# A fused attention and mixture-of-experts kernel: v of the odd early steps in the output's buffers, v of the late steps through scratch in HBM and turned as float32r

## The chip, the cores and the metric

The kernel runs on one core of one Trainium2 chip. The metric is the device time of one execution in microseconds. Three runs of the kernel before took 1270.45, 1270.66 and 1270.89 us; their median, 1270.66 us, is the number that the prediction is about. The engines are PE (matrix products), with PEld for its weight loads, ACT, DVE and POOL (elementwise work; POOL also issues the indirect transfers), and SP, which issues the plain transfers on one hardware queue.

## The reference, cut to what matters

```
# q, k, v: B=4, N=5056, C=256, float32
qn = q / (norm(q, axis=1) + 1e-6);  kn = k / (norm(k, axis=1) + 1e-6)
s  = kn.transpose(0, 2, 1) @ qn / tau            # 256 x 256 for each batch
a  = softmax(s, axis=-1)
x  = (v @ a).reshape(20224, 256)
logits = x @ w_gate + modality_bias[modality_id]  # 8 experts
e_idx  = argmax(logits, axis=1);  gate = softmax(logits)[e_idx]
for e in range(8):
    h = maximum(x[e_idx == e] @ w1[e], 0)         # 256 -> 1024
    out[e_idx == e] = gate * (h @ w2[e])          # 1024 -> 256
```

The norms and the scores sum over all tokens of a batch, so a batch's x can start only when its q and k have been read whole. A token's expert is known only when its x is there.

## The kernel before, in words

**Steps.** Each batch is cut into 10 steps of 512 tokens (the tenth is shorter), 40 steps in all, numbered g = 10 b + s. Most products are made of three float32r matmuls, high by high, low by high and high by low, where the high part is a float32r cast made by ACT and the low part the rest, subtracted by DVE.

**Gram.** `kq_pieces(b, s)` loads q and k of a step (L291), makes high and low parts (L307, L308), squares both for the norms (ACT L333, summed into acc by DVE at L335) and multiplies k by q into two PSUM banks (L344 for whole float32 operands, as in the first batch and steps 0 to 4 of batch 1; L358 and L362 for split ones). Batch 0's gram is done first, the next batch's beside the current one's steps.

**v times a.** `va_pieces(b, s)` loads v of the step (L542) into a tile with the tag "v", of which there are two buffers. `tr(h)` turns one half of the channels: four 128 x 128 transposes on PE (L559, with a float32 identity `ident`) fill one PSUM tile vtp, ACT casts it to vh (L563), DVE subtracts to vl (L564). `av(t)` multiplies (L577, 24 matmuls a step) and ACT copies the result to x (L581). `route()` finds the expert of each token (DVE L586 to L636, exp on ACT L592, the tokens' ranks by three small matmuls into rp, L613 to L615), and POOL scatters the rows of x to the list xs in HBM, sorted by expert (L499).

**Blocks.** 512 tokens of one expert are a block: weights loaded (w1r L738, w2r L742) and split (L759, L766), rows xr read back from xs (L719), turned (xtp L778, with the float32r identity `identr`), then the first product hp (L796, 12 matmuls for each of 8 parts), its relu as hh (ACT L799) and hl (DVE L800), the second product y (L814) and the scaled result yo (L830), scattered to the output by POOL (L499). yo has two buffers with the tag "yo"; the first block's yo is made after step 6.

**Order.** The pieces of a step (a block's body, v of the next step with the routing of this one, the next batch's gram) are merged by `_interleave` in the order written, and the tiling framework then sets each engine's queue by what depends on what. Instructions that depend on nothing are put early. `order(ins, others)` and `after(...)` name instructions that must come behind others; kq_pieces takes such a list as `behind`, and for batch 1's early steps it is `routed[g]`, the last instructions of a step's routing. In a queue nothing overtakes: a waiting instruction holds up what is behind it. SP issues every load of q, k, v, w1r, w2r and xr in one such order.

## Time and profile before

| | |
|---|---|
| runs, median (lowest to highest) | 1270.66 us (1270.45 to 1270.89) |
| the profiled execution | 1268.5 us |
| its span | 1266.7 us |
| PE busy | 1231.8 us, 97% of the span |
| DVE, ACT, POOL busy | 66%, 59%, 28% |
| mean granted clock of PE | 0.995 of full speed |
| hardware DMA queue (SP's loads) | 167.61 MB, 41.8% of the 16 DMA engines' time |

The profile is of one execution; its span is the time from the first to the last instruction that it shows. Rows of groups give line, engine, operation, tiles (out<-in), shapes and count, then busy time and the mean ns of one, then the idle time of the engine before them and what ended it. Rows of a timeline give start and duration in us. "x4" stands for four instructions in a row; their duration reaches from the start of the first to the end of the last, and since matmuls overlap in the pipeline, the step from one start to the next is what a stream pays. SPq is SP's queue of transfers.

### The profile page before, as it was taken

To read this page: it belongs to the slowest core of one execution; us is meant where nothing else is said; L and a number is where in the kernel's file an instruction comes from. 1 tells how busy PE (TensorE), PEld (TensorE's weight loads), DVE (VectorE), ACT (ScalarE), POOL (GpSimd) and SP (SyncE) were. 2 spreads that over 40 slices of the span, in tenths; PEclk is the share of its full clock that TensorE was granted. 3 is DMA by queue.
4 is the path that set the end of the run, shared out by engine and by line. 5 is a ranking of instruction groups with operands and counts; after the bars stand their busy time and mean duration, and the time that the engine had idled before them with its cause. 6 is when DMAs were issued, how large, how long until landed. Compare 5 with 4: busy or idle time off the path is not lost.

```text
span 1266.7 us, 23483 instructions
## 1 busy us (share of the span) xinstructions
PE 1231.8 (97%) x8226; PEld 1113.8 (88%) x8226; DVE 836.7 (66%) x2196; ACT 743.1 (59%) x1519; POOL 358.1 (28%) x344
## 2 busy tenths in 40 slices
PE   9989999999999999999999999999999999989997
PEld 8878899888988889889998998888888888879997
DVE  6788688676667766677776776565556655465452
ACT  6656568666666566676665665564555455444553
POOL 0053333222332223213332322222222333233121
PEclk9999999999999999999999999999999999999999
DMA  8869465455554555545555554434444454334320
GB/s 314 294 201 322 141 205 186 162 167 167 180 180 163 175 176 188 166 139 194 174 173 184 173 176 138 143 103 150 150 154 147 136 156 146 129 115 143 121 97 28
DMA packets 104177, 210.82 MB, mean 166 GB/s; under 512 B 11336, under 2 KB 52808, under 8 KB 104048
## 3 DMA queue, kind: packets, MB, share of 16 engines
q1 hardware_dynamic: 88304, 167.61, 41.8%
q0 software_dynamic: 15744, 41.61, 8.5%
q8 instruction: 66, 1.08, 0.4%
q14 instruction: 63, 0.52, 0.1%
HBM read 167.06 MB, written 43.43 MB: 166 GB/s over the span
## 4 chain that ended last, share of the span: by engine, by line
PE 83%; issue 8%; DVE 3%; DMA 2%; ACT 1%; POOL 1%; POOLq 0%; SPq 0%; ACTq 0%; DVEq 0%
PE y L814 30%; PE hp L796 29%; PE xp L577 10%; PE g L344 3%; PE g L358 3%; PE vtp L559 3%; PE g L362 2%; PE xtp L778 2%; DMA k<-in_k_dram 1%; POOL out_dram L499 1%; DVE hl L800 1%; DMA v<-in_v_dram 1%; PE ns L395 1%; ACT hh L799 1%; DVE acc L335 0%
## 5 line engine op out<-in xcount | busy, mean ns | idle before, releaser
L499 POOL DMA_INDIRECT xs<-x,pi x160 | 181.4, 1134 | 749.0 <-ACT w1h L759 483.1
L814 PE MATMUL y<-w2h,hh 128*128 128x256 f32 x1264 | 358.4, 284 | 6.4 <-ACT hh L799 5.2
L814 PE MATMUL y<-w2h,hl 128*128 128x256 f32 x1264 | 353.7, 280 | 2.6 <-DVE hl L800 2.2
L814 PE MATMUL y<-w2l,hh 128*128 128x256 f32 x1264 | 353.5, 280 | 0.1
L800 DVE SCALAR_TENSOR_TENSOR hl<-hp,hh 128x512 fp32r<-128x512 f32 (+1 forms) x320 | 217.0, 678 | 181.6 <-ACT hh L799 154.5
L799 ACT ACTIVATE hh<-hp 128x512 fp32r<-128x512 f32 (+1 forms) x320 | 189.9, 594 | 218.0 <-PE hp L796 147.5
L796 PE MATMUL hp<-xh,w1h 128*128 128x512 f32 (+1 forms) x640 | 256.4, 401 | 4.1 <-issue 4.1
L814 PEld LDWEIGHTS y<-w2h,hh 128*128 128x128 f32 x1264 | 237.8, 188 | 22.1 <-ACT hh L799 9.3
L796 PE MATMUL hp<-xl,w1h 128*128 128x512 f32 (+1 forms) x640 | 251.4, 393 | 0.9 <-issue 0.6
L796 PE MATMUL hp<-xh,w1l 128*128 128x512 f32 (+1 forms) x640 | 250.7, 392 | 0.3 <-issue 0.3
L814 PEld LDWEIGHTS y<-w2l,hh 128*128 128x128 f32 x1264 | 238.3, 189 | 9.2
L814 PEld LDWEIGHTS y<-w2h,hl 128*128 128x128 f32 x1264 | 237.1, 188 | 5.8 <-DVE hl L800 4.6
L499 POOL DMA_INDIRECT out_dram<-yo,xr x158 | 164.1, 1039 | 127.4 <-ACT yo L830 82.2
L766 DVE TENSOR_TENSOR w2l<-w2r,w2h 128x512 fp32r<-128x512 f32 x160 | 110.3, 689 | 66.9 <-ACT w2h L759 60.6
L796 PEld LDWEIGHTS hp<-xh,w1l 128*128 128x128 f32 x640 | 120.3, 188 | 27.2 <-issue 1.5
L759 ACT CAST w2h<-w2r 128x512 fp32r<-128x512 f32 x160 | 99.6, 622 | 70.3 <-PE y L814 54.9
L766 DVE TENSOR_TENSOR w1l<-w1r,w1h 128x512 fp32r<-128x512 f32 x160 | 110.3, 689 | 43.8 <-ACT w1h L759 37.6
L796 PEld LDWEIGHTS hp<-xl,w1h 128*128 128x128 f32 x640 | 120.7, 189 | 19.4 <-issue 5.4
L796 PEld LDWEIGHTS hp<-xh,w1h 128*128 128x128 f32 x640 | 120.4, 188 | 15.7 <-issue 2.4
L759 ACT CAST w1h<-w1r 128x512 fp32r<-128x512 f32 x160 | 100.1, 626 | 50.6 <-PE hp L796 47.0
L577 PE MATMUL xp<-ah,vh 128*128 128x264 f32 x320 | 97.7, 305 | 1.7 <-issue 0.8
L577 PE MATMUL xp<-al,vh 128*128 128x264 f32 x320 | 92.1, 288 | 0.7 <-issue 0.7
(154 smaller groups left out, 1750.3 us busy)
## 6 DMA issues: line engine op xcount, KB each, us to landing
w1r<-in_moe_w_dram SPq DMA_DIRECT2D x80, 512.0 KB
w2r<-in_moe_w_dram SPq DMA_DIRECT2D x80, 512.0 KB
xr<-xs SPq DMA_DIRECT2D x38, 516.0 KB
v<-in_v_dram SPq DMA_DIRECT2D x36, 512.0 KB
q<-in_q_dram SPq DMA_DIRECT2D x35, 512.0 KB
k<-in_k_dram SPq DMA_DIRECT2D x35, 512.0 KB
xs<-x,pi POOLq DMA_INDIRECT x160
out_dram<-yo,xr POOLq DMA_INDIRECT x158
```

Source lines behind the costliest of these rows:

```text
L344: nc.tensor.matmul(g[:, 0:C], st["k"][:pp, 2 * h + t, m * P : (m + 1) * P], st["q"][:pp, 2 * h + t, :], start=first, stop=last, skip_group ...
L358: nc.tensor.matmul(g, ks[:pp, t, m * P : (m + 1) * P], qs[:pp, t, :], start=first, stop=False, skip_group_check=True,)
L362: nc.tensor.matmul(g[:, 0:C], ks[:pp, t, C + m * P : C + (m + 1) * P], qs[:pp, t, 0:C], start=False, stop=last, skip_group_check=True,)
L499: ins = nc.gpsimd.indirect_dma_start(out=dst, out_offset=bass.IndirectOffsetOnAxis(ap=idx, axis=0), in_=rows, in_offset=None, bounds_check ...
L559: nc.tensor.matmul(tp[:, t * P : (t + 1) * P], st["v"][:, t, h * P : (h + 1) * P], ident, is_transpose=True, start=t == 0, stop=True, skip ...
L577: nc.tensor.matmul(xp[:, 0:DE], a[:, h, t * P : (t + 1) * P], w[:, h, :], start=i == 0, stop=i == len(seq) - 1,)
L759: ins = nc.scalar.copy(hi, src).ins
L766: nc.vector.tensor_tensor(lo, src, hi.bitcast(F32), ALU.subtract)
L796: nc.tensor.matmul(hp[:, 0:rows], w[:, h, fs], x[:, h, 0:rows], start=i == 0, stop=i == len(seq) - 1)
L799: nc.scalar.activation(hh[:, 0:rows], hp[:, 0:rows], AF.Relu)
L800: nc.vector.scalar_tensor_tensor(hl[:, 0:rows], hp[:, 0:rows], 0.0, hh[:, 0:rows].bitcast(F32), ALU.max, ALU.subtract)
L814: ins = nc.tensor.matmul(y, a[:, tsl], w[:, j % 2, :], start=(j == 0 and i == 0 and t % 2 == 0), stop=(j == NJ - 1 and i == 2), skip_group ...
```

## The change

It has three parts.

1. The v tile of an odd step below 6 (v_1, v_3, v_5) takes the tag "yo", the buffers of the output, which are free until the first block; the even ones keep "v".
2. `routed[g]` also holds the exp of the routing, and batch 1's gram pieces are put behind the cast and the subtraction of a turned v (`turned[...]`) as well as behind the routing.
3. For steps 12 to 39 `stage(g)` has SP copy v of the step from the input to a scratch tensor `vs{g}` in HBM, and the load reads that scratch. The tile of v is then float32r by type, and so is the PSUM tile; the transposes use `identr`. The bytes are the same; the cast and the subtraction read the PSUM tile as float32.

```diff
     cast = {}
+    turned = {}
...
+    staged = set(range(NS + 2, G))
+    vs = {
+        g: dram.tile([parts(g % NS) * TT, C], F32, name=f"vs{g}") for g in sorted(staged)
+    }
+
+    def stage(g):
+        b, s = divmod(g, NS)
+        n = parts(s) * TT
+        nc.sync.dma_start(
+            vs[g].rearrange("(p t) c -> p t c", t=TT),
+            v[b, s * STEP : s * STEP + n, :].rearrange("(p t) c -> p t c", t=TT),
+        )
...
         def load():
-            vt = p2.tile([P, TT, C], F32, tag="v", name=f"v_{g}")
+            dt = F32R if g in staged else F32
+            vt = p2.tile([P, TT, C], dt, tag="yo" if g % 2 == 1 and g < first_block else "v", name=f"v_{g}")
...
-            nc.sync.dma_start(
-                vt[:pp], v[b, t0 : t0 + pp * TT, :].rearrange("(p t) c -> p t c", t=TT)
-            )
+            src = vs[g] if g in staged else v[b, t0 : t0 + pp * TT, :]
+            nc.sync.dma_start(vt[:pp].bitcast(F32), src.rearrange("(p t) c -> p t c", t=TT))
...
-                tp = ps2.tile([P, 512], F32, tag="h" if early else "aux", name=f"vtp_{g}_{h}")
+                dt = F32R if g in staged else F32
+                tp = ps2.tile([P, 512], dt, tag="h" if early else "aux", name=f"vtp_{g}_{h}")
             for t in range(TT):
                 nc.tensor.matmul(
-                    tp[:, t * P : (t + 1) * P], st["v"][:, t, h * P : (h + 1) * P], ident,
+                    tp[:, t * P : (t + 1) * P], st["v"][:, t, h * P : (h + 1) * P], identr if g in staged else ident,
                     is_transpose=True, start=t == 0, stop=True, skip_group_check=True,
                 )
-            cast[g] = nc.scalar.copy(st["vh"][:, h, :], tp).ins
-            ins = nc.vector.tensor_tensor(st["vl"][:, h, :], tp, st["vh"][:, h, :].bitcast(F32), ALU.subtract)
+            tf = tp.bitcast(F32) if g in staged else tp
+            cast[g] = nc.scalar.copy(st["vh"][:, h, :], tf).ins
+            turned.setdefault(g, []).append(("act", cast[g]))
+            ins = nc.vector.tensor_tensor(st["vl"][:, h, :], tf, st["vh"][:, h, :].bitcast(F32), ALU.subtract)
...
+            turned[g].append(("dve", ins.ins))
...
-            nc.scalar.activation(ex, lm, AF.Exp)
+            exps = nc.scalar.activation(ex, lm, AF.Exp)
...
             routed[g] = [
+                ("act", exps.ins),
...
-            run(kq_pieces(1, s, lambda: routed[0], squares[s]))
+            run(kq_pieces(1, s, lambda: routed[0] + turned[1], squares[s]))
...
-                streams.append(list(kq_pieces(1, 2, lambda: routed[1], squares[2])))
+                streams.append(list(kq_pieces(1, 2, lambda: routed[1] + turned[2], squares[2])))
             else:
-                streams.append([f for i in (PLAN[s] if b == 0 else [s]) for f in kq_pieces(b + 1, i, routed[g - 1] if b == 0 and g > 0 else ())])
+                streams.append([f for i in (PLAN[s] if b == 0 else [s]) for f in kq_pieces(b + 1, i, routed[g - 1] + turned[g] if b == 0 and g > 0 else ())])
+        if g + 4 in staged:
+            streams[-1].insert(len(streams[-1]) // 2, lambda g=g: stage(g + 4))
```

What this does to the queues shows at three places. In the rows a number is a row's place in its engine's queue, and the last number of a tile's name is the program's own.

SP in the early steps, first before and then in the change, from the load of v_5 to the first weights of block 0 (w1r_0_0) and the first x rows (xr_0):

```order
46 L542 DMA v_5_1034<-in_v_dram 128x1024
47 L542 DMA v_6_1196<-in_v_dram 128x1024
48 L734 TENSOR_LOAD pki_0_896
...
51 L738 DMA w1r_0_0_1177<-in_moe_w1_dram 128x2x512
...
53 L742 DMA w2r_0_0_1178<-in_moe_w2_dram 128x4x256
...
57 L719 DMA xr_0_1190<-xs_129 128x1032
...
59 L738 DMA w1r_0_1_1192<-in_moe_w1_dram 128x2x512
```

```order
45 L560 DMA v_6_1224<-in_v_dram 128x1024
46 L291 DMA q_1_5_1429<-in_q_dram 128x1024
47 L291 DMA k_1_5_1431<-in_k_dram 128x1024
48 L540 DMA vs12_131<-in_v_dram 16x8192
49 L560 DMA v_7_1412<-in_v_dram 128x1024
50 L540 DMA vs13_132<-in_v_dram 16x8192
51 L540 DMA vs14_133<-in_v_dram 16x8192
52 L755 TENSOR_LOAD pki_0_924
...
55 L759 DMA w1r_0_0_1205<-in_moe_w1_dram 128x2x512
...
61 L740 DMA xr_0_1218<-xs_129 128x1032
```

v_7, which stood behind the weights of blocks 0 and 1, now stands ahead of them, with the first three copies (vs12 to vs14) around it.

SP ahead of batch 2's first q and k (q_2_0, k_2_0), where the last copies stand, before and in the change:

```order
133 L719 ISA
134 L719 DMA xr_4_2642<-xs_129 128x1032
135 L738 ISA
136 L738 DMA w1r_5_0_3102<-in_moe_w1_dram 128x2x512
137 L734 TENSOR_LOAD pki_6_2612
...
141 L291 DMA q_2_0_3174<-in_q_dram 128x1024
142 L291 DMA k_2_0_3176<-in_k_dram 128x1024
143 L542 DMA v_12_3641<-in_v_dram 128x1024
```

```order
156 L740 DMA xr_4_2671<-xs_129 128x1032
157 L540 DMA vs34_153<-in_v_dram 16x8192
158 L540 DMA vs35_154<-in_v_dram 16x8192
159 L540 DMA vs36_155<-in_v_dram 16x8192
160 L540 DMA vs37_156<-in_v_dram 16x8192
161 L540 DMA vs38_157<-in_v_dram 16x8192
162 L540 DMA vs39_158<-in_v_dram 16x7168
...
164 L759 DMA w1r_5_0_3132<-in_moe_w1_dram 128x2x512
165 L291 DMA q_2_0_3199<-in_q_dram 128x1024
...
170 L291 DMA k_2_0_3201<-in_k_dram 128x1024
...
173 L560 DMA v_12_3672<-vs12_131 128x1024
```

All 28 copies stand between rows 48 and 162, one to six at a place, though the program writes them four steps ahead of each use: nothing that they read is written by the kernel.

ACT from the second x copy of step 2 on, before and in the change (vh_4 is the cast of step 4's v, ex_2 the exp of step 2's routing, sq_1_3 are the squares of batch 1's step 3):

```order
87 L581 COPY x_2_675<-xp_2_2_826 128x264
88 L581 COPY x_2_675<-xp_2_3_834 128x264
89 L563 CAST vh_4_902<-vtp_4_0_910 128x512
90 L637 COPY x_2_675<-tokid_100 128x4
91 L333 ACTIVATE sq_1_3_0_q_917<-q_1_3_906 128x512
92 L333 ACTIVATE sq_1_3_0_k_920<-k_1_3_908 128x512
93 L592 ACTIVATE ex_2_847<-lm_2_845 128x32
94 L563 CAST vh_4_902<-vtp_4_1_923 128x512
95 L581 COPY x_3_794<-xp_3_0_930 128x264
```

```order
87 L601 COPY x_2_703<-xp_2_2_854 128x264
88 L581 CAST vh_4_930<-vtp_4_0_938 128x512
89 L601 COPY x_2_703<-xp_2_3_862 128x264
90 L581 CAST vh_4_930<-vtp_4_1_951 128x512
91 L601 COPY x_3_822<-xp_3_0_958 128x264
92 L658 COPY x_2_703<-tokid_100 128x4
93 L612 ACTIVATE ex_2_875<-lm_2_873 128x32
94 L333 ACTIVATE sq_1_3_0_q_945<-q_1_3_934 128x512
95 L333 ACTIVATE sq_1_3_0_k_948<-k_1_3_936 128x512
```

Both casts of v_4, the first x copy of step 3 and the exp of step 2 now stand ahead of the squares. On PE the three matmuls of step 2's routing (rp_2) stand behind five matmuls of xp_3_1, which came after them before.

2 lines of the change are left out of this document (1 added, 1 removed).

## The prediction

> **What bounds the kernel now.** I read the page's busy times first, then stretches of the span, then what PE waits for, then the chain of waits, and last the DMA queue of SP.
>
> ```profile
> PE 1231.8 (97%) x8226; PEld 1113.8 (88%) x8226; DVE 836.7 (66%) x2196; ACT 743.1 (59%) x1519; POOL 358.1 (28%) x344
> ...
> 50.00:100.00 50.00, 45.14 (x294) 39.79 (x294) 39.62 (x155) 31.64 (x79) 23.43 (x20) 0.97 0.74 250
> 100.00:150.00 50.00, 47.71 (x330) 43.43 (x331) 34.58 (x88) 27.02 (x54) 14.61 (x12) 1.00 0.72 239
> 150.00:200.00 50.00, 50.00 (x337) 45.66 (x337) 43.45 (x111) 38.53 (x81) 22.14 (x16) 1.00 0.59 190
> 400.00:500.00 100.00, 99.25 (x675) 90.04 (x674) 71.96 (x188) 61.64 (x125) 26.28 (x25) 1.00 0.52 168
> 700.00:800.00 100.00, 99.49 (x679) 90.64 (x679) 68.04 (x168) 59.34 (x121) 27.72 (x26) 1.00 0.51 159
> ```
>
> The columns of a stretch are its length, the busy times of PE, PEld, DVE, ACT and POOL, then PE's granted clock, the DMA share and GB/s. From 150 us on PE is busy 50.00 of 50 and over 99 of 100 us at clock 1.00, with DMA at half its capacity. So PE's own work sets the end there, and a nanosecond taken from it is a nanosecond of the total. Between 50 and 150 us PE loses 4.86 + 2.29 = 7.15 us to waits, and in the first of these stretches the clock is 0.97. These are the two places where the change can gain; the transfers of the first 200 us are where it can lose.
>
> **Part 1: turning v with the float32r identity, steps 12 to 39.** 28 steps, two groups of four transposes each: 56 groups. The kernel already turns xr in float32r, so both forms are in the trace.
>
> ```profile
> L559 PE MATMUL vtp<-ident,v 128*128 128x128 f32 x320 | 47.7, 272 | 2.2 <-DMA v<-in_v_dram 2.2
> L778 PE MATMUL xtp<-identr,xr 128*128 128x128 f32 x316 | 36.3, 237 | 0.2 <-ACT x L581 0.2
> ...
> 643.22 0.46 PE L778 MATMUL xtp<-identr,xr 128*128 128x128 f32 x4
> 643.51 0.35 PE L577 MATMUL xp<-ah,vh 128*128 128x264 f32 x1
> ...
> 658.18 0.60 PE L559 MATMUL vtp<-ident,v 128*128 128x128 f32 x4
> 658.54 0.48 PE L796 MATMUL hp<-xh,w1h 128*128 128x512 f32 x1
> ...
> 660.01 0.60 PE L559 MATMUL vtp<-ident,v 128*128 128x128 f32 x4
> 660.37 0.36 PE L814 MATMUL y<-w2h,hh 128*128 128x256 f32 x1
> ```
>
> In a full stream what counts is the time from the start of a group to the start of what follows it. It is 658.54 - 658.18 = 0.36 us, and 660.37 - 660.01 = 0.36 us, for plain float32, and 643.51 - 643.22 = 0.29 us for float32r. The saving is 0.07 us a group, 56 x 0.07 = **3.9 us**. The difference of the mean durations is 272 - 237 = 35 ns; over 224 transposes that is 7.8 us, the upper bound, though four of them overlap, so I don't take it. The lower bound is nothing: float32r may save time in xtp for a reason that v doesn't share. The weight loads, the ACT cast and the DVE subtraction behind the transposes are the same instructions as before.
>
> A rule beside it: the Trainium skill (TensorE: Matmul & The Clock Gate, Back-to-back issue gap) gives 81 ns per 128-column matmul in a stream of weight loads and matmuls, without regard to the type. By it a group would take 0.32 us and the part would save 0.04 x 56 = 2.2 us, an estimate; xtp's 0.29 us, 72 ns each, already goes below it here.
>
> **Part 2: the early steps.** v_1, v_3 and v_5 get the output's two buffers, so that v_6 and v_7 wait in SP for v_2's and v_4's transposes instead of v_4's and v_5's. In the order of the change the squares of batch 1 stand behind the casts of the next v, and the route's matmuls move behind some of xp.
>
> ```profile
> 75.34 0.18 PE L613 MATMUL rp<-oh,trim 128*128 128x32 bf16 x1 [1.88 <-DVE sm L632]
> ...
> 76.00:78.00 2.00, 2.00 (x13) 1.97 (x12) 1.86 (x14) 1.20 (x3) 0.18 (x1) 0.70 0.09 31
> 78.00:80.00 2.00, 2.00 (x10) 1.95 (x9) 2.00 (x7) 0.52 (x2) 1.69 (x2) 0.50 0.18 66
> ...
> 66.00 7.60 SPq L542 DMA_DIRECT2D v<-in_v_dram  x2
> 92.40 0.88 SPq L542 DMA_DIRECT2D v<-in_v_dram  x2
> ...
> 92.40 8.99 DMA v<-in_v_dram
> 101.52 0.74 PE vtp L559 x5
> ...
> 99.41 1.06 ACT L799 ACTIVATE hh<-hp 128x512 fp32r<-128x512 f32 x2
> 99.45 0.23 DVE L600 TENSOR_TENSOR oh<-val,vm 128x32 bf16<-128x32 f32 x1
> ```
>
> Three losses stand there. *The wait for v_7*: SP issued it at 92.40, into full DMA engines, and PE stood until 101.52, 2.17 us by the view of waits below. In the new order it goes out before the weights of block 0, some 20 us earlier. What is late next is the one-hot vector oh, done at 99.68, and the two hh, done at 100.47 (in the new order the first of them no longer stands behind a square): PE would then wait to about 99.7 to 100.5 instead of 101.52, a gain of 1.0 to 1.8 us. *The wait at rp_2*, 1.88 us: the order puts five more xp matmuls and the x copies ahead of it, so some of the time is filled, but the route's own chain on DVE is as long as before; I take half, 0.9. *The half clock*: 0.70 and 0.50 between 76 and 80 us, on the heels of that wait, cost 2 x 0.30 + 2 x 0.50 = 1.6 us of full speed. If PE stands less, this can go altogether; I take half, 0.8. Sum 1.3 + 0.9 + 0.8 = 3.0, and with smaller waits that lie on the same path:
>
> ```profile
> PE vtp L559 <- DMA v<-in_v_dram: 2.2, 1, 2.2
> PE rp L613 <- DVE sm L632: 1.9, 1, 1.9
> PE rp L613 <- DVE vm L598: 0.6, 1, 0.6
> PE xp L577 <- ACT x L581: 0.5, 1, 0.5
> PE xp L577 <- DVE vl L564: 0.5, 1, 0.5
> ```
>
> (half of the last three, 0.8) gives **3.8, taken as 3.5 us** since a shorter early part also brings xr_0 closer, which waits for scatters of x. Bounds: all rows and the clock, 5.7 + 1.6 = 7.3 us, and nothing, if each wait is only replaced by another.
>
> The Trainium skill (TensorE: Matmul & The Clock Gate, Why this matters for your kernels) has the clock fall to half after about 3 us without matmuls between bursts. Here it fell behind a pause of 1.88 us, so the trace agrees in kind and shows a shorter pause; by that rule the whole 1.6 us would return once the pause is cut, an estimate of 0.8 us more than the sum.
>
> **Part 3: the copies of v to scratch.** 28 transfers within HBM of 512 KB each (448 in the short steps), issued by SP, are new work for the DMA engines. They depend on nothing, so the order has them all between SP's rows 48 and 162, that is between about 73 and 187 us of the old trace.
>
> ```profile
> q1 hardware_dynamic: 88304, 167.61, 41.8%
> ...
> 60.00:190.00 130.00, 122.93 (x818) 110.28 (x817) 102.16 (x318) 81.75 (x179) 51.72 (x43) 0.99 0.67 220
> 90.00:100.00 10.00, 8.07 (x50) 6.17 (x48) 9.78 (x44) 8.99 (x22) 6.72 (x6) 1.00 1.02 357
> 100.00:110.00 10.00, 8.48 (x62) 7.96 (x63) 8.15 (x28) 6.89 (x13) 3.90 (x4) 1.00 1.03 384
> 150.00:160.00 10.00, 10.00 (x68) 8.99 (x68) 9.57 (x36) 8.24 (x20) 4.33 (x4) 1.00 0.23 85
> 180.00:190.00 10.00, 10.00 (x68) 8.97 (x67) 8.36 (x34) 6.68 (x15) 3.48 (x3) 1.00 0.28 85
> ...
> 160.02 0.35 SPq L291 DMA_DIRECT2D q<-in_q_dram  x1
> 182.25 0.61 ACT L307 CAST qs<-q 128x512 fp32r<-128x512 f32 x1
> ...
> 177.38 0.37 SPq L719 DMA_DIRECT2D xr<-xs  x1
> 187.34 0.38 SPq L738 DMA_DIRECT2D w1r<-in_moe_w_dram  x1
> 193.55 0.34 SPq L291 DMA_DIRECT2D k<-in_k_dram  x1
> 198.79 0.64 ACT L333 ACTIVATE acc<-k 128x512 f32<-128x512 f32 x1 [0.18 <-DMA k<-in_k_dram]
> ```
>
> The hardware queue moved 167.61 MB in 41.8% of the span of 1266.7 us, 317 GB/s; a full stretch moved 357 to 384. At 317 a copy of 0.52 MB takes 1.65 us, all 28 take 46 us. No copy within HBM is in the trace, so this is a bound from the nearest row; if reading and writing each took that time, 92 us. Idle DMA time between 60 and 190 us is 130 x (1 - 0.67) = 43 us. So the copies roughly fill what is free there, and push loads back by a few us each. Most loads have room: q of batch 1's step 8, say, is issued at 160.02 and used at 182.25, 22 us later. The tight one is the first k of batch 2, issued at 193.55 and used at 198.79. Six copies go out behind xr at 177.38, ahead of w1r at 187.34: 6 x 1.65 = 10 us of transfer in a stretch of 10 us with 0.28 busy, so they end some 3 us into the next loads. ACT would stand about that long; PE has other work then (50.00 of 50 busy). I put the cost at **1 us**, bounds nothing and one load of batch 2 or of a block that lands 5 us late. From step 12 on v itself is read from scratch instead of the input, the same bytes in the same shape: nothing. SP's issue time, about 0.35 us each, lies in its waits for buffers.
>
> **Sum.** -3.9 - 3.5 + 1.0 = **-6.4 us**. The profiled execution took 1268.5 us, its span 1266.7; that makes 1262.1 and a span of 1260.3. The runs' median is 1270.66, 2.2 above the profiled one, so the forecast for the median is 1264.3.
>
> **The rivals.**
>
> *A, the transposes alone (chance 0.22).* Early waits give way to others: hh and oh are ready only 1 to 2 us before v_7, and the route's chain is as long. For it speaks that ACT and DVE are busy 0.90 and 0.98 of 90 to 100 us; against it, that the longest waits are for a transfer and for one chain. 1270.66 - 3.9 + 0.5 = about 1267.3.
>
> *B, the larger gain (0.18).* float32r saves the 35 ns of the durations, or the whole 7.3 us of the early part returns: 3.9 + 7.3 = 11.2, or 7.8 + 3.5 = 11.3; about 1260. Against it speak the starts in the stream and the replaced waits.
>
> *C, the copies choke the early loads (0.10).* Place: from 90 to 110 us, where DMA is at 1.02 and 1.03, and at the first step of batch 2. With copies of double price, 92 us of transfer in 43 us of room, about 49 us run over, and each load in SP's queue stands behind those issued before it. The row `92.40 8.99` shows that a load into a full queue takes 9 us, so I count two such loads on PE's path at about half of that, 10 us at double price. Slower than before it becomes when PE stands more than the 7.4 us of gains, so, on a line from 1 us at my price to 10 at double, with copies beyond 1.7 times my price; at double, 10 - 7.4 = +2.6 us: 1273.3.
> The Trainium skill (DMA: Bandwidth & Descriptors, Queues, rings and completion order) says that one engine's loads and copies share one ring on each DMA engine and are taken in its order, so a load behind six copies waits for all six. That speaks for C; the rows of 90 to 110 us agree, as loads there land late though nothing but older transfers stands ahead.
>
> *D, float32r is no faster for v (0.10).* The transposes may be paced by their weight loads, which don't change; xtp's shorter step would then come from its neighbours. Then only -3.5 + 1.0 = -2.5 us is left: 1268.2.
>
> **How the numbers follow.** My forecast has 0.40, as against A 0.22, B 0.18, C 0.10, D 0.10. About 0.2%, 2.5 us, is what a measurement here can tell from no change. Forecast and B lie below 1268.1, most of A too, D on the bound: faster 0.40 + 0.18 + 0.14 + 0.03 = 0.75. The rest of A, most of D, and a mild C lie within: 0.08 + 0.06 + 0.03 = 0.17. C beyond it: 0.08. The range runs from B's 1259 to D and the start of C, 1269.5.
>
> **What will show it.** vtp of the late steps with a mean near 237 ns and 0.29 us to the next start; PE busy some 4 us less; the wait of vtp for v gone from the view of waits, 1 us or less in its place; clock 1.00 between 76 and 80 us; DMA share near 0.95 from 70 to 190 us, and k of batch 2 landing by 202. The prediction falls if the copies take over 3 us each, if PE waits for weights or xr before 200 us, or if groups of vtp stay at 0.36 us.

## The result, and the profile after

The change is slower. In the first comparison it took 1287.01 us (median of four runs, 1281.33 to 1292.29), the kernel before 1270.56 us (1266.58 to 1270.89): ratio 1.0133, 95% interval 1.0095 to 1.0171. Forecast were 1264.3 us, with 1259 to 1269.5 as the range. The profiled execution after took 1281.33 us, 12.8 more than the profiled one before.

The same views as before, of the kernel after: the busy times and SP's hardware queue from the page, then the stretches (length, busy PE, PEld, DVE, ACT and POOL, granted clock, DMA share, GB/s).

```profile
PE 1237.6 (97%) x8226; PEld 1113.3 (87%) x8226; DVE 836.6 (65%) x2196; ACT 743.8 (58%) x1519; POOL 357.7 (28%) x344
...
q1 hardware_dynamic: 89200, 182.10, 44.3%
```

```profile
50.00:100.00 50.00, 44.97 (x294) 40.13 (x294) 37.01 (x148) 29.40 (x73) 21.41 (x19) 0.93 0.72 252
60.00:190.00 130.00, 121.36 (x793) 108.67 (x793) 97.18 (x309) 80.17 (x175) 47.94 (x41) 0.96 0.87 308
150.00:200.00 50.00, 50.00 (x339) 45.54 (x338) 42.14 (x108) 37.13 (x78) 21.07 (x14) 1.00 0.91 324
400.00:500.00 100.00, 99.09 (x681) 90.35 (x680) 71.42 (x180) 61.84 (x127) 26.85 (x24) 1.00 0.52 168
700.00:800.00 100.00, 98.03 (x658) 87.98 (x658) 68.48 (x168) 60.38 (x122) 32.21 (x32) 1.00 0.52 163
```

The copies are there: DMA 0.87 busy between 60 and 190 us instead of 0.67, and 0.91 between 150 and 200 us instead of 0.59. But PE does not stand for loads; between 150 and 200 us it is busy throughout. Two other things are worse: the clock between 50 and 100 us is 0.93, not 0.97, and between 700 and 800 us, where no copy runs any more, PE is idle for 1.97 us instead of 0.51. The transposes themselves did what the sum says. Here is a group of the change in the timeline, and its row on the page:

```profile
668.47 0.46 PE L576 MATMUL vtp<-identr,v 128*128 128x128 f32 x4
668.77 0.46 PE L817 MATMUL hp<-xh,w1h 128*128 128x512 f32 x1
...
670.23 0.46 PE L576 MATMUL vtp<-identr,v 128*128 128x128 f32 x4
670.52 0.35 PE L835 MATMUL y<-w2h,hh 128*128 128x256 f32 x1
```

```profile
L576 PE MATMUL vtp<-identr,v 128*128 128x128 f32 x224 | 25.7, 237 | 0.0
```

From start to next start it is 0.30 and 0.29 us, where plain float32 took 0.36. So some 4 us were gained, and over 16 lost elsewhere. What PE waits for, the largest rows:

```profile
PE y L835 <- ACT hh L820: 9.3, 9, 2.4
PE hp L817 <- issue: 5.6, 12, 1.0
PE y L835 <- issue: 5.2, 10, 0.9
PE y L835 <- DVE hl L821: 3.9, 17, 0.3
PE xp L597 <- ACT x L601: 3.3, 1, 3.3
```

The wait of vtp for v (2.2 us before) is gone, but y waits 9.3 us for hh. Before it was 5.2:

```profile
PE y L814 <- ACT hh L799: 5.2, 7, 1.7
```

Three of these waits in the timeline of PE of the change, and the stretches right behind them:

```profile
73.66 0.59 PE L597 MATMUL xp<-ah,vh 128*128 128x264 f32 x1 [3.26 <-ACT x L601]
...
141.99 0.39 PE L835 MATMUL y<-w2h,hh 128*128 128x256 f32 x1 [2.39 <-ACT hh L820]
...
583.15 0.39 PE L835 MATMUL y<-w2h,hh 128*128 128x256 f32 x1 [1.64 <-ACT hh L820]
```

```profile
72.00:76.00 4.00, 2.35 (x11) 2.35 (x12) 0.82 (x3) 1.74 (x4) 0.14 (x1) 0.50 0.10 33
76.00:80.00 4.00, 4.00 (x19) 3.37 (x19) 2.12 (x13) 2.01 (x6) 0.00 (x0) 0.65 1.02 369
143.00:148.00 5.00, 5.00 (x26) 4.58 (x26) 1.55 (x3) 1.27 (x4) 0.00 (x0) 0.66 0.93 322
584.00:588.00 4.00, 4.00 (x20) 3.92 (x21) 2.24 (x4) 1.79 (x5) 0.00 (x0) 0.57 0.31 90
```

Behind each of the three the clock is at half for a while, and that costs about as much again: at 143 to 148 us 0.34 x 5 = 1.7 us. Comparing the starts of the 40 steps in the two traces (by ACT's first cast vh of each step), the change is 1.1 us behind at step 8, 3.7 at step 9 (the wait at 141.99), 3.7 at step 22, 8.6 at step 23 (the wait at 583.15), 12.6 at step 30, and 14.6 at step 39.

What does ACT do before such a wait? The first of them, as POOL, PE and ACT show it:

```profile
61.60 1.30 POOL L500 DMA_INDIRECT xs<-x,pi  x1 [49.99 <-ACT x L601]
...
71.17 0.98 POOL L500 DMA_INDIRECT xs<-x,pi  x1 [0.30 <-issue]
...
70.11 0.28 PE L597 MATMUL xp<-ah,vl 128*128 128x264 f32 x1
...
73.22 0.38 ACT L601 COPY x<-xp 128x264 f32<-128x264 f32 x1 [3.91 <-remote]
```

The last matmul for this x ended at 70.39. ACT was idle, and yet the copy started only at 73.22. In between POOL issued eight scatters in an unbroken row, from 61.60 to 72.15; the copy followed 1.07 us after the last. "remote" says that the trace has no releaser for it. I call this a **late release**: an instruction whose input is ready and whose engine is idle starts some us late. The two hh of the other rows are of this kind too. The kernel before has late releases as well: in most blocks (22 of blocks 1 to 37), hh of part 2 (hh_2) starts 3 us or more after its matmuls (a part of hp has six of them, not the twelve named with the blocks above); summed over these blocks of the profiled execution that is 87.9 us, after the change 95.3. PE has other work most of that time: before it idles 8.4 us for y in these blocks, after the change 18.4. So the question was what makes PE idle more, and what makes the releases late.

### The profile page after: what moved, and what is told of

It is laid out like the page before. It is cut to its first block, busy times and chain, and to the rows that moved or that the text cites. A ratio compares the mean times of both kernels' runs of the same rounds, so it can differ in the third digit from the quotient of the medians.

```text
span 1279.6 us, 23503 instructions
## 1 busy us (share of the span) xinstructions
PE 1237.6 (97%) x8226; PEld 1113.3 (87%) x8226; DVE 836.6 (65%) x2196; ACT 743.8 (58%) x1519; POOL 357.7 (28%) x344
## 3 DMA queue, kind: packets, MB, share of 16 engines
q1 hardware_dynamic: 89200, 182.10, 44.3%
## 4 chain that ended last, share of the span: by engine, by line
PE 90%; issue 3%; DVE 3%; ACT 1%; another core or an unknown queue 1%; DMA 1%; POOL 1%; POOLq 0%; SPq 0%; DVEq 0%; ACTq 0%
PE y L835 34%; PE hp L817 32%; PE xp L597 10%; PE g L358 4%; PE g L344 3%; PE vtp L576 2%; PE g L362 2%; PE xtp L799 2%; DVE hl L821 1%; ACT hh L820 1%; DMA k<-in_k_dram 1%; PE ns L395 1%; POOL out_dram L500 1%; DVE acc L335 0%
## 5 line engine op out<-in xcount | busy, mean ns | idle before, releaser
L500 POOL DMA_INDIRECT xs<-x,pi x160 | 177.9, 1112 | 765.4 <-ACT w1h L780 402.3
L835 PEld LDWEIGHTS y<-w2h,hh 128*128 128x128 f32 x1264 | 238.2, 188 | 32.3 <-ACT hh L820 14.6
L500 POOL DMA_INDIRECT out_dram<-yo,xr x158 | 167.2, 1058 | 126.1 <-ACT yo L851 80.6
L780 ACT CAST w1h<-w1r 128x512 fp32r<-128x512 f32 x160 | 100.1, 625 | 51.6 <-PE hp L817 41.8
```

What stands on the lines that cost most here:

```text
L500: ins = nc.gpsimd.indirect_dma_start(out=dst, out_offset=bass.IndirectOffsetOnAxis(ap=idx, axis=0), in_=rows, in_offset=None, bounds_check ...
L780: ins = nc.scalar.copy(hi, src).ins
L835: ins = nc.tensor.matmul(y, a[:, tsl], w[:, j % 2, :], start=(j == 0 and i == 0 and t % 2 == 0), stop=(j == NJ - 1 and i == 2), skip_group ...
```

## The experiments

There are six comparisons, each with its own runs of the kernel before on the same chip. In three of them the kernel before took 1270.6, 1283.0 and 1273.9 us and its releases (or those of the kernels beside it) were late; in the other three it took 1235.1, 1235.3 and 1235.3 us, and there are next to no late releases in any trace (4 to 14 us in all). I call the first *late* and the others *prompt* comparisons. What the expectations say of a chip with hh late or in time is this difference. Ratios are to the kernel before of the same comparison, with the 95% interval.

### The parts by themselves (a prompt comparison)

e1 is parts 1 and 2 alone: one line of the change is different.

```diff
-    staged = set(range(NS + 2, G))
+    staged = set()
```

> Parts 1 and 2 alone: v of the odd early steps in the output's buffers and the new early order; no copies, v of all steps turned as float32. If the copies or the turning make the loss, this is 1266 to 1270 us, at or below the kernel before (1270.6); if the early order or the buffers make it, 1277 or more, with the half clock at 72 us and the late steps 0.4 us longer each.

e2 is the whole change with v turned as float32, so that the copies are there and the quicker turning isn't:

```diff
-            dt = F32R if g in staged else F32
+            dt = F32
...
-                dt = F32R if g in staged else F32
+                dt = F32
...
-                    tp[:, t * P : (t + 1) * P], st["v"][:, t, h * P : (h + 1) * P], identr if g in staged else ident,
+                    tp[:, t * P : (t + 1) * P], st["v"][:, t, h * P : (h + 1) * P], ident,
```

> The change with the copies to scratch and v read from there, but turned as float32. If the copies make the whole loss, 1284 to 1292 us (the gain of the transposes is missing too); if the turning makes the late loss, only what is lost up to step 12 stays, 1272 to 1276 us.

e3 is part 3 alone: the copies and the float32r turning, with the early buffers and the order of the squares as before.

```diff
-            vt = p2.tile([P, TT, C], dt, tag="yo" if g % 2 == 1 and g < first_block else "v", name=f"v_{g}")
+            vt = p2.tile([P, TT, C], dt, tag="v", name=f"v_{g}")
...
-            run(kq_pieces(1, s, lambda: routed[0] + turned[1], squares[s]))
+            run(kq_pieces(1, s, lambda: routed[0], squares[s]))
```

> Part 3 and the turning alone: early buffers and order as before. If copies or turning make the loss, 1280 to 1290 us; if the early order or the buffers make it, 1266 to 1270 us.

e4 is the whole change, with each copy put behind the latest load of v in SP's queue, so that about one goes out a step:

```diff
+    loaded = {}
...
-        nc.sync.dma_start(
+        ins = nc.sync.dma_start(
             vs[g].rearrange("(p t) c -> p t c", t=TT),
...
+        order(ins.ins, [loaded[max(loaded)]])
...
-            nc.sync.dma_start(vt[:pp].bitcast(F32), src.rearrange("(p t) c -> p t c", t=TT))
+            loaded[g] = nc.sync.dma_start(vt[:pp].bitcast(F32), src.rearrange("(p t) c -> p t c", t=TT)).ins
```

> The change with each copy held in SP's queue behind the load of v three steps ahead of its own, so one copy a step instead of 28 between 61 and 190 us. If the early crowd of copies makes the loss, 1262 to 1268 us; if the turning makes the late loss, 1274 to 1280 us; if each copy costs PE wherever it is, 1280 or more.

Measured, with the kernel before at 1235.1 us: e1 1230.76 (0.9958, 0.9941 to 0.9974), e2 1229.6 (0.9956, 0.994 to 0.9973), e3 1233.09 (0.9982, 0.9972 to 0.9992), e4 1226.07 (0.992, 0.9903 to 0.9936). The times that I had expected were for a kernel before at 1270.6 us, so none of them could come true. Here every part gains or costs nothing against before: the early part 4.3 us, copies added to it nothing that can be told, the turning, from e4 against e1, 4.7. Part 3 alone (e3) gains 2.0, less than the turning brings: its trace has PE waiting 5.05 us for a v at 100.66, and 6.8 us of half clock there. The starts of the steps of e4 against e1 show it as a slope: 0.9 us ahead at step 11, 5.3 at step 39, 4.4 us over the 28 steps. Forecast were 3.9. None of the four explains the loss, and all waits of PE for y were under 1 us. So the loss belonged to something that this comparison didn't have.

### The change and the kernel before once more (a late comparison)

e5 is the change, unaltered; e6 the kernel before, for a second profile; e7 the change with scratch rows of 4 KB for each partition, so that a copy is cut into 128 rows of that size.

```diff
-        g: dram.tile([parts(g % NS) * TT, C], F32, name=f"vs{g}") for g in sorted(staged)
+        g: dram.tile([parts(g % NS), TT * C + 32], F32, name=f"vs{g}") for g in sorted(staged)
...
```

> The change itself again, beside the kernel before, on the chip of this call. In the first comparison ACT started hh about 3 us late once a block in both kernels, and later in the change; the runs of the change's parts show no such lateness, and the kernel before takes 1235 us there. If that lateness belongs to the chip and moment of the first comparison, the change is 1226 to 1230 us against 1235 (the predicted -6.4 us within 3 us). If the parts are harmless alone and the crowd of copies together with the float32r turning is what loses, it is 1245 us or more.

> The kernel before, for its profile on this chip. If the lateness of hh belongs to the first chip, PE waits for hh under 1 us in all, the clock keeps 1.00 after 150 us, and the stretch of a late step is 27.0 us instead of 28.0; the early waits (v_7, rp_2) stay as in the first profile. If it belongs to the kernel, the hh rows are late here too.

> The change with each copy cut into rows of 4 KB (scratch rows padded by 128 bytes, 128 rows a copy) instead of 16 pieces of 32 KB. If long pieces hold up other transfers (instruction loads, scatters), this is 2 us or more faster than the change; if only the bytes count, within 1 us of it.

Before took 1283.04 us. e5 was 1298.88 (1.0132, 1.0099 to 1.0164), e7 1294.75 (1.0114, 1.0065 to 1.0163); e6's one profiled execution took 1287.87. So the loss came back with its size, and the shape of the copies isn't its cause: e7 is 4.1 us under e5, less than the runs of either lie apart (8 and 13 us), and still 11.7 over before. In the starts of the steps e5 is 7.3 us *ahead* of e6 at step 9 and 8.1 at step 22, and then loses, to 8.1 behind at step 39 and 9.3 in the spans, long after the last copy went out (183.7 us). PE's idle time for y in blocks 1 to 37 was 21.8 us in e5 and 11.4 in e6.

What is different so late in the program? The line that inserts the copy as one more piece into the last of the merged lists. `_interleave` takes the pieces of a list at even spacing, so a list with one more piece has all its pieces at other places. The copy costs PE nothing, but the pieces around it move. PE's order in block 15, first without the extra piece (the rows of e1), then with it (those of e9, described below, whose PE order is the change's):

```
3383 L817 MATMUL hp_3_8143<-xh_7780,w1h_1_7886 128x512
3389 L358 MATMUL g_3_7556<-qs_1_0_8079,ks_1_0_8080 128x512
3391 L358 MATMUL g_3_7557<-qs_1_0_8079,ks_1_0_8080 128x512
3393 L358 MATMUL g_3_7556<-qs_1_0_8079,ks_1_0_8080 128x512
3395 L358 MATMUL g_3_7557<-qs_1_0_8079,ks_1_0_8080 128x512
3397 L835 MATMUL y_15_8098<-w2h_1_7890,hh_2_8119 128x256
3403 L835 MATMUL y_15_8099<-w2h_1_7890,hh_2_8119 128x256
3409 L597 MATMUL xp_1_8190<-ah_7619,vh_7672 128x264
```

```
3383 L817 MATMUL hp_3_8143<-xh_7780,w1h_1_7878 128x512
3389 L835 MATMUL y_15_8098<-w2h_1_7882,hh_2_8119 128x256
3395 L835 MATMUL y_15_8099<-w2h_1_7882,hh_2_8119 128x256
3401 L597 MATMUL xp_1_8182<-ah_7627,vh_7672 128x264
3407 L358 MATMUL g_3_7551<-qs_1_0_8071,ks_1_0_8072 128x512
```

Without it eight gram matmuls (g, every second one shown) stand between hp_3 and the y that needs hh_2, and they fill PE's time while hh_2 is late. With it they stand behind that y, and PE idles (583.15 above is this place). The same eight matmuls move in blocks 4 to 23, but PE idles only where hh_2 is later than the work that is left in front of that y: in the change hh_2 is 5.5 us late in block 15, at most 3.4 in the others of these blocks. In the last batch, where the last list is that of v itself, it is xp and with it the routing that move, so the scatters of x come at another time.

### The extra piece apart from the copies

e8 is the change with the copy issued just before the merge instead of as a piece in it. Row for row, PE's order is then that of e1.

```diff
-            streams[-1].insert(len(streams[-1]) // 2, lambda g=g: stage(g + 4))
+            stage(g + 4)
```

e9 is the opposite: e1, without copies and turned as float32, with a piece that does nothing where the change has its copy. Row for row, PE's order is that of the change.

```diff
-        if g + 4 in staged:
-            streams[-1].insert(len(streams[-1]) // 2, lambda g=g: stage(g + 4))
+        if g + 4 >= NS + 2 and g + 4 < G:
+            streams[-1].insert(len(streams[-1]) // 2, lambda: None)
```

e10 is e8 with the copies behind the loads of v, as in e4. e11 is e10 with one wait added: the four scatters of a block's output (blocks 0 to 35) wait for the last matmul of part 4 of the next block, so that POOL issues four scatters in a row and not eight. All other queues keep e10's order.

```diff
+            if j == AT and st.get("put") is not None:
+                for t in range(TT):
+                    after(st["put"](t), [mm.ins])
...
```

> The change with one line different: the copy is issued just before the pieces of a step are merged, not as an extra piece in the last of the merged lists, so PE's order is that of the early part alone, with the copies and the float32r turning in full. On a chip where hh of a block's part 2 starts over 1 us late (the first comparison's, and that of e5): if the extra piece in the merge is the cause, 4 to 10 us under the kernel before (ratio 0.992 to 0.997), PE's waits for y in blocks 1 to 37 back to 9 to 12 us from 18 to 22; if the copies' transfers or the float32r turning are, about the change's +13 to +16 us (1.010 to 1.013). On a chip where hh is in time: both say 2 to 6 us under before (0.995 to 0.998), as with e3, whose copies went out early too.

> The early part alone (no copies, v from the input, float32 turning), with a piece that does nothing put in the last of the merged lists where the change has its copy: PE's order is that of the change in every row. On a chip with late hh: if the extra piece is the cause, +4 to +12 us against before (1.003 to 1.010; it has the early part's gain of 5 to 7 us, but not the turning's 4), PE's waits for y 16 to 22 us; if copies or turning are, 4 to 8 us under before (0.994 to 0.997). On a chip with hh in time: 3 to 6 us under before either way, since there the order of y and gram matmuls makes no wait.

> As e8, and each copy ordered in SP's queue behind the latest load of v, so that one goes out a step and not all in the first 190 us. If the extra piece made the loss and the early burst of copies only costs what e3 and e4 showed: 1 to 4 us under e8, so 7 to 13 us under before on any chip (0.990 to 0.995). If the copies made the loss by their mere number, it stays near the change's +13 to +16 us on a chip with late hh.

> As e10, with the four scatters of a block's yo (blocks 0 to 35) made to wait for the last matmul of part 4 of the next block, some 15 us later than they would go; every other queue has the same order. POOL then issues four scatters in a row, not eight. If the unbroken row of eight scatters is what makes PE's signals late, hh of part 2 starts within 0.6 us of its matmuls (sum of lateness over blocks 1 to 37 under 25 us from about 100), PE's waits for y fall under 4 us, and the time is 8 us or more under e10 on a chip with late hh. If the lateness has another source, it stays at 80 to 110 us and the time within 3 us of e10. On a chip with hh in time, within 1.5 us of e10.

This comparison was a prompt one (before 1235.34 us), so it could not tell the theories apart: e8 1226.64 (0.9931, 0.9918 to 0.9945), e9 1230.72 (0.9963, 0.995 to 0.9977), e10 1226.4 (0.9924, 0.9911 to 0.9938), e11 1226.78 (0.9934, 0.992 to 0.9947). It shows that where releases are prompt the extra piece costs nothing (e9 gains 4.6 us, as e1 gained 4.3) and that without it the change's parts bring 8.7 to 8.9 us, more than the 6.4 forecast. The change itself was never run in a prompt comparison.

So e8, e9 and e11 were run again beside the change.

> The kernel of e8 again, to be seen where hh of a block's part 2 starts late. There: 4 to 10 us under before (0.992 to 0.997) and PE's waits for y in blocks 1 to 37 at 9 to 12 us, if the extra piece in the merge makes the change's loss; +13 to +16 us (1.010 to 1.013) if copies or turning do. Where hh is in time: 0.993 as before.

> The kernel of e9 again. Where hh is late: +4 to +12 us against before (1.003 to 1.010) and waits for y of 16 to 22 us, if the extra piece makes the loss; 0.994 to 0.997 if copies or turning do. Where hh is in time: 0.996 as before.

> The kernel of e11 again. Where hh is late in the kernel before: if the unbroken row of eight scatters makes PE's signals late, hh's lateness falls from about 100 us to under 25 us, waits for y under 4 us, and the time is 8 us or more under e12; if not, within 3 us of e12. Where hh is in time: 0.993 as before.

> The change itself again. Where hh is late: 1.010 to 1.015 as in the two comparisons so far. Where hh is in time, it was not run yet: the copies' early burst and the extra piece cost nothing measurable there (e8 and e10 are equal, e9 equals e1), so 0.993 to 0.995, 6 to 9 us under before.

This comparison was a late one (before 1273.89 us, 1265.02 to 1278.37):

| | us | ratio | idle for y, blocks 1 to 37 | lateness of hh_2 |
|---|---|---|---|---|
| e12, copies and turning, no extra piece | 1272.87 | 1.0006 (0.9976 to 1.0035) | 10.2 us | 92.4 us |
| e13, extra piece alone | 1290.06 | 1.0129 (1.0093 to 1.0165) | 22.5 us | 97.0 us |
| e15, the change | 1287.12 | 1.0099 (1.0065 to 1.0133) | 19.9 us | 98.0 us |
| e14, e10 with the scatters parted | 1234.89 | 0.9691 (0.9658 to 0.9724) | 1.1 us | 8.4 us |

**The extra piece makes the loss.** e15 and e12 differ in nothing but where the copy is issued, as a piece or ahead of the merge: 1287.12 against 1272.87, 14.3 us, with intervals that don't overlap. e13 has no copy and no float32r turning, only a piece that does nothing, and it is as slow as the change, although it contains the early part. e12 has both copies and turning and loses nothing. The theory that copies or turning make the loss wanted e13 at 0.994 to 0.997 and e12 at 1.010 or more; both fell elsewhere. Two expectations of mine failed too: e13 was to be 4 to 12 us over before and is 16.2 over; and e12 was to be 4 to 10 us under before, and its interval allows 3 us at most. Its profiled execution was the quickest of its ten runs (1267.43), the traces of before come from other comparisons, and so it stays open where the gain of 8.7 us went that the same kernel, as e8, has where releases are prompt.

PE's idle time for y by blocks, us, in every profile of a late comparison with the scatters as they were, first the kernels without the extra piece and then those with it (the orders differ in blocks 2 to 29):

| blocks | before | e6 | e12 | change | e5 | e7 | e15 | e13 |
|---|---|---|---|---|---|---|---|---|
| 1 | 0.8 | 2.4 | 0.9 | 2.6 | 1.7 | 0.9 | 2.3 | 2.3 |
| 5 | 0.1 | 0.2 | 0.1 | 0.0 | 1.6 | 1.6 | 0.0 | 2.7 |
| 15 | 0.0 | 0.1 | 0.5 | 1.9 | 2.0 | 1.9 | 2.9 | 1.3 |
| 25 | 1.3 | 1.9 | 0.6 | 1.7 | 1.9 | 1.6 | 1.5 | 1.7 |
| 26 to 30 | 1.5 | 1.2 | 1.5 | 5.3 | 7.3 | 8.0 | 6.8 | 6.7 |
| 31 to 37 | 4.8 | 5.0 | 6.1 | 4.4 | 5.1 | 4.4 | 5.2 | 5.9 |
| all others | 0.0 | 0.6 | 0.5 | 2.5 | 2.2 | 3.1 | 1.2 | 1.9 |

Blocks 1, 25 and 31 to 37 differ as much within a group as between the groups: the wait at 141.99, in block 1, is one that the kernel before has too in e6. Blocks 15 and 26 to 30 and the others part the groups cleanly: 5 to 8 us against 1.2 to 1.5 in blocks 26 to 30 alone.

Block 29 is one of them. The first and last scatter on POOL, then hh_2 on ACT and y on PE; first e12, then e13.

```profile
982.11 1.30 POOL L500 DMA_INDIRECT xs<-x,pi  x1 [17.72 <-ACT w1h L780]
...
991.43 0.98 POOL L500 DMA_INDIRECT out_dram<-yo,xr  x1 [0.30 <-issue]
...
993.67 0.60 ACT L820 ACTIVATE hh<-hp 128x512 fp32r<-128x512 f32 x1 [3.73 <-PE xp L597]
...
995.05 0.39 PE L835 MATMUL y<-w2h,hl 128*128 128x256 f32 x1 [0.22 <-DVE hl L821]
```

```profile
1003.41 0.98 POOL L500 DMA_INDIRECT xs<-x,pi  x1 [21.15 <-issue]
...
1012.64 0.98 POOL L500 DMA_INDIRECT out_dram<-yo,xr  x1 [0.30 <-issue]
...
1014.92 0.60 ACT L820 ACTIVATE hh<-hp 128x512 fp32r<-128x512 f32 x1 [5.87 <-PE hp L817]
...
1015.57 0.39 PE L835 MATMUL y<-w2h,hh 128*128 128x256 f32 x1 [2.10 <-ACT hh L820]
```

The matmuls of hp_2 end at about 990.5 in e12 and at 1010.0 in e13. In both, hh_2 starts 1.3 us after the last scatter is issued. In e13 the row of scatters ends 1.7 us later relative to the matmuls, hh_2 is 4.9 us late instead of 3.2, and PE has run out of work. Then the clock falls, at this place and in two other blocks of that batch (e13):

```profile
896.00:901.00 5.00, 4.78 (x20) 4.11 (x21) 2.43 (x4) 1.62 (x4) 0.00 (x0) 0.66 0.27 105
985.00:990.00 5.00, 5.00 (x24) 4.42 (x25) 1.89 (x4) 1.49 (x4) 0.00 (x0) 0.66 0.31 110
1016.00:1021.00 5.00, 4.78 (x21) 4.30 (x21) 2.14 (x4) 1.61 (x4) 0.00 (x0) 0.66 0.31 107
```

Five such stretches of 0.34 x 5 = 1.7 us each in e13 (two more lie at 139 and 272 us) against one in e12 make 6.8 us, and idle time for y 12.3 more: 19.1 us, where the two spans (1287.0 and 1265.6) are 21.4 apart. That is no full account, since other idle time of PE fell: by the busy times of the two pages (1239.9 and 1226.9) all its idle time grew by 8.4 us, so that with the 6.8 some 6 us are left over, in the busy time. Block 1 and the stretch at 139 us, 1.4 + 1.7 us, are chance in this; the medians are 17.2 us apart.

**The row of eight scatters makes the releases late.** e14 differs from e12 in two things, the scatters parted and the copies behind the loads of v. The copies can't be what makes hh late: the kernel before and e13 have none and are late too. e14's block 29 has four scatters in a row, and hh_2 (the second hh here) starts right when its matmuls end, at 968.0:

```profile
959.61 1.30 POOL L501 DMA_INDIRECT xs<-x,pi  x1 [5.57 <-ACT w1h L783]
...
963.78 0.98 POOL L501 DMA_INDIRECT xs<-x,pi  x1 [0.30 <-issue]
...
965.48 0.60 ACT L826 ACTIVATE hh<-hp 128x512 fp32r<-128x512 f32 x1
968.00 0.60 ACT L826 ACTIVATE hh<-hp 128x512 fp32r<-128x512 f32 x1 [1.44 <-PE hp L820]
```

Its view of waits has nothing left of hh but 0.9 us, and two steps take 53.70 us of full PE instead of 56.00 (stretches of the same two steps, e14 and then e12):

```profile
PE xp L599 <- ACT x L603: 3.5, 2, 3.3
...
PE y L841 <- ACT hh L826: 0.9, 2, 0.7
```

```profile
990.90:1044.60 53.70, 53.70 (x375) 49.35 (x374) 33.26 (x91) 29.27 (x61) 16.73 (x17) 1.00 0.44 148
```

```profile
1014.50:1070.50 56.00, 54.87 (x376) 49.40 (x375) 33.53 (x91) 29.30 (x61) 16.84 (x17) 1.00 0.43 141
```

(56.00 - 53.70) / 2 = 1.15 us a step. Over some 34 steps with a block that would be 39 us, but not every step pays as much: from step 10 to step 39 e12 falls 25.9 us further behind, the two spans are 32.8 us apart and the medians 38. Only 56.00 - 54.87 = 1.13 of the 2.30 us shows as idle time; the rest is in the busy time of about as many matmuls at the same clock. (In the rows of vtp above a group is 0.46 us long and the next starts after 0.30, so a stall of up to 0.16 us leaves no idle time.) e14 is still 7.4 us over the same kernel in a prompt comparison (e18 below). The 3.3 us that are left in its first row stand behind two groups of x scatters early on, eight in a row, which e14 doesn't part. Between e11 and e10, where releases are prompt, the same wait changed nothing.

### The scatters parted in the kernel before and in the change

e16 is the kernel before with that wait, e17 the change with it, e18 the kernel of e14 again.

> The kernel before with the scatters of yo of blocks 0 to 35 made to wait for part 4 of the next block, nothing else. Where hh is late in the kernel before: if the row of eight scatters is the whole cause, the time falls to about 1240 to 1246 us, what the kernel before takes where no signal is late (1235) and some us more, a ratio of 0.970 to 0.982; if the scatters only matter together with the change's own parts, it stays within 1% of before. Where hh is in time: 0.998 to 1.002.

> The change with the same delay of the scatters. If the loss is only the meeting of the extra piece in the merge with late signals, it is 5 to 9 us faster than e16 (the prediction's sum was 6.4), 1231 to 1239 us where before takes 1270 or more, and 1226 to 1231 where before takes 1235. If the extra piece or the copies cost by themselves, no faster than e16.

> The kernel of e14 again, beside e16 and e17. Copies out of the burst and no extra piece: equal to e17 or up to 3 us faster; where hh is late in the kernel before, 0.967 to 0.975; else 0.992 to 0.995.

The comparison was a prompt one (before 1235.26 us): e16 1234.24 (0.9996, 0.9987 to 1.0005), e17 1231.36 (0.9963, 0.995 to 0.9977), e18 1227.45 (0.9936, 0.9922 to 0.9949). So what parting the scatters brings to the kernel before alone, where releases are late, was not measured. e17 shows something else: it is 2.9 us under e16, not the 5 to 9 that were expected, and 3.9 above e18, not 3 at most. Its view of the starts has it 1.0 us ahead of e18 at step 10 and 4.4 behind at step 11. SP and ACT there (e17):

```profile
179.48 3.59 SPq L540 DMA_DIRECT2D vs<-in_v_dram  x5
183.31 0.38 SPq L760 DMA_DIRECT2D w1r<-in_moe_w_dram  x1
184.36 0.36 SPq L291 DMA_DIRECT2D q<-in_q_dram  x1
...
197.20 0.63 ACT L333 ACTIVATE acc<-q 128x512 f32<-128x512 f32 x1 [6.42 <-DMA q<-in_q_dram]
197.74 0.58 ACT L824 ACTIVATE hh<-hp 128x512 fp32r<-128x512 f32 x1
```

The first q of batch 2 goes out right behind six copies (the first of them at 178.93) and its square starts 12.8 us later; ACT stands for 6.42 us, hh stands behind it in ACT's queue, and PE waits 2.5 us for hh and then runs 3.4 us at half clock. This is the place that the prediction's part 3 names, at 5.4 us instead of 1: ACT stands as it says, by q and not k, but PE has no other work then. The Trainium skill (DMA: Bandwidth & Descriptors, Queues, rings and completion order) has a load wait for the transfers ahead of it on the same ring; this row agrees. It is a matter of timing, though: in the change (first comparison) the same q went out at 195.17, 9.8 us after the last copy, and ACT waited 1.4 us.

## Why the prediction was wrong

**The failed step is part 3's term for the copies, +1.0 us, and with it the sum: it has nothing for the order of the blocks.** Part 3 prices a copy as a transfer: new work for the DMA engines, loads that land late, SP's issue time. But the copy is also a piece in a merged list, and moves gram, xp and routing around it in blocks 2 to 29. I had looked at the queues in the early part only. The line that makes it a piece costs 14.3 us where releases are late (e15 against e12); e13 against e12 gives 17.2, with the turning's gain on e12's side.

**That is not the whole miss.** In that comparison the change is 13.2 us over before, 19.6 from the forecast's -6.4. The extra piece is 14.3 of it; the other 5.4 are the gain that e12 lacks, -1.0 instead of -6.4, and stay open.

**The condition under which it costs was in the profile of before.** It has 5.2 us of y waiting for hh, the largest wait of PE there; none of the parts dealt with it. I treated blocks as a full stream because PE was busy for 99.25 of 100 us. It was so only since other matmuls happened to stand where hh_2 is late by 3 us and more. A stream that is full in the order of before says nothing of the stream in another order. Nor was that busy time all work: e16, whose rows on PE are those of before, one for one, has this on its page, taken where releases are prompt:

```profile
PE 1217.8 (99%) x8226; PEld 1112.6 (90%) x8226; DVE 835.0 (68%) x2196; ACT 746.1 (61%) x1519; POOL 358.3 (29%) x344
```

The same 8226 matmuls are busy for 14.0 us less than in before. The half clock (two stretches of 3.4 us in before, one in e16) makes 1.7 of that. So "PE's own work sets the end" was read out of a number that held stalls too.

**The terms.** *Turning*, -3.9: measured -4.4 in the slope of e4 against e1; 0.29 to 0.30 us a group, mean 237 ns. The mechanism and the size were right, and rival D is out. The Trainium skill's 81 ns for each matmul would give 0.32 us a group (TensorE: Matmul & The Clock Gate, Back-to-back issue gap); the trace has 0.30 or less. *Early part*, -3.5: about right, measured -4.3 where releases are prompt (e1); in the profile of the first comparison it was lost to the late x copy at 73.22 and the half clock behind it, and the change was 1.1 us behind at step 8. That half clock, at 72 to 79 us, took the place of the one at 76 to 80 of which I had half gone. It comes and goes between executions (e6, the kernel before, has one at 74 us, e12 none). *Copies*, +1.0: nothing that can be told between e8 and e10 or e1 and e2, but 5.4 us in e17, where the q load fell right behind them, a little over the bound of one load 5 us late; what decides is when that q goes out. The queue's share of its span went from 41.8% of 1266.7 to 44.3% of 1279.6 us, which is 37 us for 28 copies, 1.3 us each, under the 1.65 of the prediction.

Where releases are prompt, e4, e8 and e10, which have all three gains and are freed of either the extra piece or the burst, are 8.7 to 9.0 us under before. The sum of -6.4 was a fair account, 2.3 to 2.6 us small, of what the parts do there, and no account of what the change does in the kernel that it was made for, whose releases are late.

**The rivals.** C, slower by choked loads, had the sign but not the mechanism: between 60 and 150 us PE waited for no load. A (transposes alone), B (a larger gain) and D were all of the other sign. A rival that asked what the extra piece does to the merge would have been the right one; the 0.08 for slower came from C alone. (By small slips C's shares add up to 0.11 and D's to 0.09, where both have 0.10.)

**What would make it wrong**, by its own list, were copies of over 3 us, waits for weights or xr before 200 us, and groups of vtp at 0.36 us. None came true, with a copy at 1.3 us of the engines' time. Of the signs that were to show it, vtp's row and the end of its wait for v came; PE's busy time rose by 5.8 us instead of falling by 4, and the clock from 76 to 80 us was 0.65 instead of 1.00. Nothing in either list looks for waits behind 202 us.

## What to carry to other kernels

An instruction that costs nothing can still be dear if it is added to a list that is merged by position: compare the whole queue of the engine that sets the end, not only the place of the edit, and give every y, hh or the like that moves nearer to what it waits for a price. A long wait that is covered by other work is a debt: before moving work, list what covers it. And when a loss can't be found in any part of a change, put a no-op in its place, and take the edit out by that line alone: e13 and e12 settled what the parts by themselves could not.

The best kernel measured is that of e14 and e18: the early part, copies behind the loads of v and outside the merge, v turned as float32r, and the output's scatters parted from those of x: 0.9691 where releases are late. Where they are prompt it has 0.9936, level with e4, e8, e10 and e11 (0.992 to 0.9934). What parting the scatters alone brings to the kernel before where releases are late stays unmeasured.

## What the runs showed of the hardware

- **Eight indirect transfers issued in a row by POOL, one every 1.28 us, can hold up the release of other engines** until about 1.1 to 1.3 us after the last (73.22 against 72.15; 993.67 against 992.41; 1014.92 against 1013.62). With four in a row hh was late by 8.4 us in all instead of 92.4, and the kernel ran in 1234.9 us instead of 1272.9 (with its copies elsewhere, too). By what path it happens, the trace does not say ("remote").
- **It does not happen always.** The same kernel took 1235 us in three comparisons, without late releases, and 1271 to 1283 in three others. Chip number 12 was in both kinds, so it is not a matter of the chip alone; what sets it stays open.
- **Short pauses can halve the clock.** PE idle times of 2.39, 1.64 and 2.10 us were each followed by about 3.4 us at 0.5, 1.7 us lost. Others as long were not: 2.17 us in the kernel before (the wait for v up to 101.52), 2.67 us in e15 (up to 582.64). The Trainium skill (TensorE: Matmul & The Clock Gate, Why this matters for your kernels) speaks of about 3 us without matmuls; here less was enough at times.
